# The first 512 columns of w_in in one pair of transfers, and the first chunk of batch 0's P in one run of 512 columns with both copies on ScalarE

## The chip, the cores and the metric

The kernel runs on one core of a Trainium2 chip. The metric is the device time of one execution in microseconds, as the median of several runs. Five engines work side by side: TensorE (PE in the profile, with its weight loads as PEld), VectorE (DVE), ScalarE (ACT), GpSimd (POOL) and SyncE (SP). Each takes its instructions in program order and waits at an instruction until the data and the buffers that it needs are there. Transfers are issued from the queues of POOL, SP and ACT, and run on 16 DMA engines.

## What is computed

Eight batches of attention between 512 tokens and 32 state vectors, in 8 heads of 64 columns, in both directions, and a dense block with an exact Gelu on the result:

```python
def _attn_ref(x, state):
    B, H, S, D = x.shape                    # 8, 8, 512, 64; state has 32 rows
    scale = 1.0 / np.sqrt(D)
    scores = scale * np.matmul(x, state.transpose(0, 1, 3, 2))
    ...
    a = np.exp(scores)
    a /= a.sum(-1, keepdims=True) + 1e-09
    xread = np.matmul(a, state)
    scores2 = scale * np.matmul(state, x.transpose(0, 1, 3, 2))
    ...
    sread = np.matmul(a2, x)
    return np.concatenate([xread, sread], axis=2)

def _moe_ref(x, w_in, w_out):               # x: 4352 x 512, w_in: 512 x 2048, w_out: 2048 x 512
    h = x @ w_in
    g = 0.5 * h * (1.0 + erf(h * inv_sqrt2))
    return g @ w_out
```

## The kernel before

**The product P.** For the token rows, `xread @ w_in` equals `a @ (state @ w_in)`, head by head. So the kernel first forms, for each batch, P = state @ w_in: a tile of 128 partitions by 2 halves t by 2048 columns, where half t holds four heads of 32 state rows each. It is made in chunks of 512 columns (`p_mm`, L435: for each of four head positions c and two halves t a matmul of 64 rows by 32 columns, so eight matmuls side by side) into two PSUM banks, and copied to SBUF as bf16. Then hp = P^T a^T gives 128 of the 2048 hidden columns for all 512 tokens at a time: two matmuls, t = 0 and t = 1, add into one bank (`mm1`, L501; for the first four of batch 0 `first`, L1112). ScalarE applies Gelu to hp and writes g, and TensorE multiplies g with w_out (`mm2_m`, L544, for batch 0).

**The start.** The order on every engine is written out by hand, from L1074 on. Batch 0 is loaded in four quarters q by SP and ScalarE queues as float32 and cast on chip; its scores, exponentials, sums and the normalized weights `a` follow quarter by quarter (`scores0`, `sums0`, `norm0`); `norm0(0)` gives the t = 0 half of `a`, `norm0(1)` the t = 1 half. `atr` (L363) transposes one half of `a` with four TensorE transposes into a PSUM bank; for batch 0 the t = 0 half is copied to SBUF (tile AT) by ScalarE and the t = 1 half by VectorE (L375, L376).

**The POOL queue.** All weights, the state of batches 1 to 7 and x of batches 1 to 7 are loaded through the POOL queue, with a cast from float32 to bf16 in the transfer. The order at the start is L126 to L131, then `load_x(1)` (L1096), then `load_rest` (L134). `load_w_in(f0, f1)` (L103) issues two transfers, one for each half t: 256 rows by f1 - f0 columns, which land on 64 partitions in four pieces each.

**The stretch around the change.** The first 512 columns of w_in come in two pairs of transfers of 256 columns. `pmat00(h)` (L480) makes half h of the first chunk of P of batch 0: eight matmuls of 256 columns into two PSUM tiles. On ScalarE it copies the t = 0 part, and for h = 0 the t = 1 part too. For h = 1 the t = 1 part stays in PSUM (`late`) until VectorE copies it at L1124, after the copy of AT's t = 1 half. Between these stand calls of `keep_warm(n)` (L146): matmuls on a tile of zeros, of n times 128 columns in all, that give TensorE work to do. After `first`, ScalarE runs the Gelu of four hp tiles (L1130), ahead of which the program loads ScalarE's table for that function.

**The PSUM banks.** Four banks, o0 to o3, are given out in turn by `otile` (L55) through a counter, `turn`; the next user of a bank waits until the one before has been read. Four more (`ftile`) hold hp and other products. Before `mm2_m(0, 0)` the counter is set to 3 (L1131).

**What follows.** From L1132 on: the products with w_out, a second burst of P chunks (`burst`, L1136, which needs w_in's columns 512 to 1024), then `xtr(1, ...)` (L1141), 32 TensorE transposes of x of batch 1, which need `load_x(1)` landed, and so on through the eight batches.

Of the kernel before, what the change touches and what calls it, by code (L numbers as in the profile page):

```python
# [10 lines left out]
BF16 = mybir.dt.bfloat16  # L11
# [6 lines left out]
def kernel(  # L18
# [8 lines left out]
    nc = tc.nc  # L27
# [3 lines left out]
    d_model, d_ff = moe_w_in.shape  # L31
    SB = S + NS
    scale = 1.0 / math.sqrt(D)
    HC = H // 2
# [6 lines left out]
    att = ctx.enter_context(tc.tile_pool(name="att", bufs=2))  # L41
# [11 lines left out]
    turn = [0]  # L53

    def otile(shape, name, at=None):  # L55
        if at is None:
            at = turn[0] % 4
            turn[0] += 1
        return ps_o.tile(shape, FP32, name=name, tag=f"o{at}")
# [6 lines left out]
    w_in_bf = persist.tile([128, HC, d_ff], BF16, name="w_in_bf")  # L66
    w_out_bf = persist.tile([128, MC, d_model], BF16, name="w_out_bf")
    ident = persist.tile([128, 128], BF16, name="ident")
    sbd = persist.tile([128, B, HC, 2 * NS], BF16, name="sbd")
# [33 lines left out]
    def load_w_in(f0, f1):  # L103
        for t in range(2):
            nc.gpsimd.dma_start(  # L105
                out=w_in_bf[64 * t:64 * t + 64, :, f0:f1],
                in_=moe_w_in[256 * t:256 * t + 256, f0:f1].rearrange("(c d) f -> d c f", c=HC),
            )
# [3 lines left out]
    def load_w_out(m0, m1):  # L112
        nc.gpsimd.dma_start(out=w_out_bf[:, m0:m1, :], in_=w_out_r[:, m0:m1, :])  # L113
# [9 lines left out]
            in_=st_rows[:, b0:b1, :, :].rearrange("q b t d -> q (b t) d"),  # L123
        )

    load_w_in(0, 256)  # L126
    load_w_in(256, 512)
    load_w_out(0, 2)
    load_st(1, 2)
    load_w_out(2, 4)  # L130
# [15 lines left out]
    def keep_warm(n):  # L146
        ps = otile([128, 512], "warm_ps")
        while n > 0:
            w = 128 * min(n, 4)
            nc.tensor.matmul(  # L150
                ps[:, 0:w], lhsT=warm[:, 0:128], rhs=warm[:, 0:w], start=True, stop=True
            )
            n -= 4
# [209 lines left out]
    def atr(b, ts=(0, 1)):  # L363
        A = atts[b]
        if 0 in ts:
            A.AT = att.tile([128, SJ, 2, 128], BF16, name="AT", tag="AT")
        for t in ts:
            if b == 0:
                ps = ps_o.tile([128, SJ, 128], BF16, name="aT_ps", tag=f"o{turn[0] % 4}")
                turn[0] += 1  # L370
            else:
                ps = ps_f.tile([128, SJ, 128], BF16, name="aT_ps", tag="f")
            for j in range(SJ):
                nc.tensor.transpose(ps[:, j, :], A.a[:, 2 * j + t, :], ident)
            copy = nc.scalar.copy if b == 0 and t == 0 else nc.vector.tensor_copy  # L375
            copy(out=A.AT[:, :, t, :], in_=ps)  # L376
# [56 lines left out]
    Ps = {}  # L433

    def p_mm(b, f, tiles):  # L435
        if b not in Ps:
            Ps[b] = att.tile([128, 2, d_ff], BF16, name="P", tag="P")
        ps = [tiles([128, 512], "p_ps") for t in range(2)]
        for c in range(HC):
            for t in range(2):  # L440
                nc.tensor.matmul(  # L441
                    ps[t][32 * c:32 * c + 32, :],
                    lhsT=sbd[64 * t:64 * t + 64, b, c, 32 * t:32 * t + 32],
                    rhs=w_in_bf[64 * t:64 * t + 64, c, f * 512:(f + 1) * 512],
                    start=True,
                    stop=True,
                )
        return ps
# [28 lines left out]
            p_copy(*x)  # L477


    def pmat00(h):  # L480
        if h == 0:
            Ps[0] = att.tile([128, 2, d_ff], BF16, name="P", tag="P")
        ps = [otile([128, 256], "p_ps") for t in range(2)]
        for c in range(HC):
            for t in range(2):
                nc.tensor.matmul(
                    ps[t][32 * c:32 * c + 32, :],
                    lhsT=sbd[64 * t:64 * t + 64, 0, c, 32 * t:32 * t + 32],
                    rhs=w_in_bf[64 * t:64 * t + 64, c, 256 * h:256 * h + 256],
                    start=True,  # L490
                    stop=True,
                )
        nc.scalar.copy(out=Ps[0][:, 0, 256 * h:256 * h + 256], in_=ps[0])
        if h == 0:
            nc.scalar.copy(out=Ps[0][:, 1, 0:256], in_=ps[1])
        return ps


    gs = {}
# [600 lines left out]
    norm0(1)  # L1100
    load_rest()
    keep_warm(2)
    pmat00(0)
    keep_warm(8)
    atr(0, (0,))
    keep_warm(4)
    late = pmat00(1)

    gs[0] = gpool.tile([128, MC, S], BF16, name="g", tag="g")
    hps = [ps_f.tile([128, S], FP32, name="hp", tag="f") for m in range(4)]  # L1110
# [10 lines left out]

    first(0, (0, 1))
    atr(0, (1,))
    nc.vector.tensor_copy(out=Ps[0][:, 1, 256:512], in_=late[1])  # L1124
    for q in range(4):
        ones0(q)
    first(0, (2, 3))
# [94 lines left out]
    for b in range(2, B):  # L1222
        nb = b + 1
        for p in range(8):
# [16 lines left out]
            late = p == 5 and b % 2 and nb < B  # L1241
# [115 lines left out]
```

## Time and profile before

| | us |
|---|---|
| median of 3 runs (lowest, highest) | 201.96 (201.9, 202.41) |
| the profiled execution | 202.25 |
| its span, from the first to the last instruction | 200.3 |
| TensorE busy | 193.9 (97%) |
| VectorE busy | 155.1 (77%) |
| ScalarE busy | 145.6 (73%) |
| GpSimd busy | 48.1 (24%) |
| granted TensorE clock | 1.00 in all of the span |

Each line of a timeline gives the start, the time taken, the engine, the line of the kernel, the operation, the tiles written and read, shapes and the number of instructions merged; in brackets the idle time before it and what ended it. Lines overlap, since matmuls are pipelined and an instruction can begin before the one ahead has been written back. "Us to landing" of a transfer runs from its issue to its arrival.

### The profile page before, as it was taken

The numbers are of one execution on the slowest core, as the hardware profiler recorded it, in microseconds if no ns is written. First come the engines' busy times: TensorE is split into PE (matmuls) and PEld (weight loads), VectorE is DVE, ScalarE is ACT, GpSimd is POOL, SyncE is SP. The second block draws the span as 40 slices with busy tenths as digits, with TensorE's granted clock in tenths as the row PEclk, the third lists the DMA queues.
The fourth block names the chain that finished last, engine by engine and source line by source line (L and its number), as shares of the span: only waits on it lengthen the run. The fifth ranks groups of instructions, "written<-read, shape, count | busy, mean of one in ns | idle before, by whom it ended". The sixth has DMA issues, their size and how long they took to land.

```text
span 200.3 us, 5055 instructions
## 1 busy us (share of the span) xinstructions
PE 193.9 (97%) x2102; PEld 134.3 (67%) x2107; DVE 155.1 (77%) x279; ACT 145.6 (73%) x264; POOL 48.1 (24%) x65
## 2 busy tenths in 40 slices
PE   7899999999999999999999999999999999999993
PEld 2533544465767777767777787677776888878893
DVE  2963796969989769975997798849966897984863
ACT  3785577699896799569966997599948778775120
POOL 8972504543403444040504300030000000000000
PEclk9999999999999999999999999999999999999999
DMA  5999999976494959680797025420024010030044
GB/s 192 197 174 202 206 199 201 183 136 142 84 149 77 241 65 164 141 214 0 77 188 209 5 67 95 138 75 27 28 107 106 0 55 0 7 153 0 18 146 157
DMA packets 40567, 23.16 MB, mean 116 GB/s; under 512 B 21856, under 2 KB 39136, under 8 KB 40544
## 3 DMA queue, kind: packets, MB, share of 16 engines
q0 software_dynamic: 13984, 8.10, 29.9%
q1 hardware_dynamic: 25728, 14.22, 27.5%
q10 hardware_dynamic: 832, 0.52, 0.8%
q8 instruction: 16, 0.26, 0.5%
q14 instruction: 7, 0.06, 0.1%
HBM read 17.30 MB, written 8.91 MB: 131 GB/s over the span
## 4 chain that ended last, share of the span: by engine, by line
PE 86%; DMA 5%; POOL 4%; ACT 2%; issue 0%; DVE 0%; POOLq 0%
PE xp L647 36%; PE hp L506 26%; DMA xb<-in_x_dram 5%; PE xp L727 5%; PE op L548 3%; PE sp L866 3%; PE rp L932 3%; POOL w_in_bf L105 2%; PE op L532 2%; PE xp L773 2%; PE pt L333 2%; ACT P L1002 1%; PE p_ps L441 1%; PE sr L962 1%; POOL sbd L95 1%; POOL w_out_bf L113 1%
## 5 line engine op out<-in xcount | busy, mean ns | idle before, releaser
L513 ACT ACTIVATE g<-hp 128x512 bf16<-128x512 f32 x124 | 67.1, 614 | 17.0 <-PE hp L506 16.8
L506 PE MATMUL hp<-AT,P 128*128 128x512 bf16 x248 | 62.2, 379 | 0.0
L647 PEld LDWEIGHTS <-gsum 128*128 128x128 bf16 x416 | 40.4, 98 | 8.9 <-issue 0.4
L647 PE MATMUL xp<-ws,gsum 128*128 128x256 bf16 x320 | 38.2, 273 | 0.0
L506 PEld LDWEIGHTS <-P 128*128 128x128 bf16 x248 | 23.0, 98 | 19.4 <-ACT P L452 0.7
L647 PEld LDWEIGHTS <-g 128*128 128x128 bf16 x240 | 23.3, 98 | 4.8
L637 DVE TENSOR_TENSOR gsum<-g 128x2048 bf16<-128x2048 bf16 x14 | 17.0, 1218 | 0.6 <-ACT g L513 0.6
L225 POOL COPY x<-xb 128x1024 bf16<-128x1024 bf16 x12 | 12.2, 1044 | 18.5 <-DMA xb<-in_x_dram 18.5
L235 POOL COPY xo<-xb 128x1024 bf16<-128x1024 bf16 x12 | 12.2, 1043 | 14.1 <-PE sr L962 13.9
L647 PE MATMUL xp<-w_out_bf,g 128*128 128x256 bf16 x128 | 15.3, 273 | 0.0
L647 PE MATMUL xp<-ws,g 128*128 128x256 bf16 x112 | 13.4, 273 | 0.0
L1016 POOL COPY hold<-g 128x1 bf16<-128x1 bf16 x7 | 2.3, 334 | 42.9 <-ACT g L513 42.9
L666 DVE TENSOR_TENSOR c<-qb 128x256 f32<-128x256 f32 x6 | 2.6, 425 | 12.7 <-ACT qb L749 12.7
L548 PE MATMUL op<-w_out_bf,g 128*128 128x512 bf16 x44 | 11.0, 380 | 0.5 <-issue 0.3
L647 PE MATMUL xp<-w_out_bf,gsum 128*128 128x256 bf16 x96 | 11.5, 273 | 0.0
L666 DVE TENSOR_TENSOR oh<-xp,c 128x512 f32<-128x512 f32 x14 | 9.6, 686 | 2.4 <-PE xp L647 2.0
L1002 DVE CAST P<-p_ps 128x512 bf16<-128x512 f32 x15 | 9.4, 683 | 2.4 <-PE p_ps L441 2.4
L356 DVE TENSOR_TENSOR a<-e,ics 128x512 bf16<-128x512 bf16 x14 | 10.5, 750 | 0.5
L353 DVE TENSOR_REDUCE cs<-e 128x16 f32<-128x512 bf16 x14 | 9.5, 678 | 0.9 <-ACT e L340 0.9
L513 ACT ACT_TABLE_LOAD x7 | 9.0, 1283 | 0.1
L441 PE MATMUL p_ps<-w_in_bf,sbd 64*32 64x512 bf16 x248 | 9.0, 380 | 0.0
L637 DVE TENSOR_TENSOR gsum<-gsum,g 128x2048 bf16<-128x2048 bf16 x7 | 8.6, 1225 | 0.2
(155 smaller groups left out, 308.9 us busy)
## 6 DMA issues: line engine op xcount, KB each, us to landing
out_dram<-oh SPq DMA_DIRECT2D x15, 256.0 KB, 3.3
xb<-in_x_dram POOLq DMA_DIRECT2D x7, 512.0 KB, 7.1
out_dram<-oh SPq DMA_DIRECT2D x6, 512.0 KB, 3.1
w_in_bf<-in_moe_w_in_dram POOLq DMA_DIRECT2D x6, 256.0 KB, 11.7
out_dram<-osb SPq DMA_DIRECT2D x5, 256.0 KB, 3.0
w_out_bf<-in_moe_w_out_dram POOLq DMA_DIRECT2D x4, 256.0 KB, 7.8
w_out_bf<-in_moe_w_out_dram POOLq DMA_DIRECT2D x2, 512.0 KB, 13.3
x0f<-in_x_dram SPq DMA_DIRECT2D x3, 256.0 KB, 3.8
```

The costliest lines, as they stand in the source:

```text
L225: nc.gpsimd.tensor_copy(out=A.x4[:, :, :, 64 * t:64 * t + 64].rearrange("p j c d -> p c j d"), in_=src[:, t],)
L235: eng.tensor_copy(out=A.xo[:, :, :, 2 + 64 * t:66 + 64 * t].rearrange("p j c d -> p c j d"), in_=src[:, t],)
L356: nc.vector.tensor_tensor(out=A.a[:, :, hs].rearrange("p g (c n) -> p g c n", n=NS), in0=e4, in1=ics[:, :, :].to_broadcast((128, G, 2, NS) ...
L441: nc.tensor.matmul(ps[t][32 * c:32 * c + 32, :], lhsT=sbd[64 * t:64 * t + 64, b, c, 32 * t:32 * t + 32], rhs=w_in_bf[64 * t:64 * t + 64, c ...
L506: nc.tensor.matmul(hp, lhsT=Ps[b][:, t, m * 128:(m + 1) * 128], rhs=atts[b].AT[:, :, t, :], start=(t == 0), stop=(t == 1),)
L513: nc.scalar.activation(out=gs[b][:, m, :], in_=hp, func=AF.Gelu)
L548: nc.tensor.matmul(ops[b, j], lhsT=gs[b][:, m, j * 128:(j + 1) * 128], rhs=w_out_bf[:, m, :], start=(m == 0), stop=(m == MC - 1),)
L637: nc.vector.tensor_tensor(out=got[name], in0=x, in1=y, op=op)
L647: nc.tensor.matmul(ps[:, j - js[0], :], lhsT=lhs[:, m, 128 * j:128 * j + 128], rhs=rhs[:, m, :], start=(first and j == js[0] and m == 0), ...
L666: nc.vector.tensor_tensor(out=out, in0=x, in1=y, op=ALU.add)
L727: nc.tensor.matmul(xs[b, 0][:, at, :], lhsT=lhs[:, m, :], rhs=rhs[:, m, :], start=(start and m == 0), stop=(m == MH // 2 - 1), skip_group_ ...
L1002: copy(out=Ps[b][:, t, f * 512:(f + 1) * 512], in_=ps[t])
```

## The change

`load_w_in(0, 512)` takes the place of `load_w_in(0, 256)` and `load_w_in(256, 512)`: two transfers on the POOL queue in place of four, each with twice as many columns. `pmat00` loses its argument: it calls `p_mm(0, 0, otile)`, so eight matmuls of 512 columns make the whole chunk, and ScalarE copies the t = 0 part at once. The t = 1 part stays in its bank until a second ScalarE copy, which now stands after the AT copy of the t = 0 half, so VectorE's copy at L1124 is gone. The counter `turn` is moved on by one, past the bank that holds this part. The warm-up matmuls, 12 times 128 columns in all, are four before and eight after `atr(0, (0,))`; before they were eight and four.

```diff
-    load_w_in(0, 256)
-    load_w_in(256, 512)
+    load_w_in(0, 512)
     load_w_out(0, 2)
     load_st(1, 2)
     load_w_out(2, 4)
@@
-    def pmat00(h):
-        if h == 0:
-            Ps[0] = att.tile([128, 2, d_ff], BF16, name="P", tag="P")
-        ps = [otile([128, 256], "p_ps") for t in range(2)]
-        for c in range(HC):
-            for t in range(2):
-                nc.tensor.matmul(
-                    ps[t][32 * c:32 * c + 32, :],
-                    lhsT=sbd[64 * t:64 * t + 64, 0, c, 32 * t:32 * t + 32],
-                    rhs=w_in_bf[64 * t:64 * t + 64, c, 256 * h:256 * h + 256],
-                    start=True,
-                    stop=True,
-                )
-        nc.scalar.copy(out=Ps[0][:, 0, 256 * h:256 * h + 256], in_=ps[0])
-        if h == 0:
-            nc.scalar.copy(out=Ps[0][:, 1, 0:256], in_=ps[1])
-        return ps
+    def pmat00():
+        ps = p_mm(0, 0, otile)
+        nc.scalar.copy(out=Ps[0][:, 0, 0:512], in_=ps[0])
+        return ps[1]
@@
     keep_warm(2)
-    pmat00(0)
+    late = pmat00()
+    keep_warm(4)
+    atr(0, (0,))
     keep_warm(8)
-    atr(0, (0,))
-    keep_warm(4)
-    late = pmat00(1)
+    nc.scalar.copy(out=Ps[0][:, 1, 0:512], in_=late)
+    turn[0] += 1
@@
     first(0, (0, 1))
     atr(0, (1,))
-    nc.vector.tensor_copy(out=Ps[0][:, 1, 256:512], in_=late[1])
     for q in range(4):
         ones0(q)
     first(0, (2, 3))
```

## The prediction

> **What bounds the kernel now.** I read the clock and span first (one core, span 200.3 us, granted clock 1.000), then the chain of work that ended last, the waits of TensorE, the timelines of the engines from 8 to 20 us, and the transfer rate by stretches. The profiled execution took 202.25 us, 1.95 us more than its span; the median of the runs is 201.96, so 0.29 us comes off any sum made in this profile.
>
> The chain, in order of time (start, us, what), where the change touches it:
>
> ```profile
> 3.05 2.65 POOL w_in_bf L105 x4
> 5.70 0.71 POOL w_out_bf L113
> ...
> 7.82 1.19 POOL w_in_bf L105 x2
> 9.01 10.36 DMA xb<-in_x_dram
> 19.36 0.04 issue
> 19.41 1.08 PE xT_ps L271 x32
> ```
>
> From 19.41 to the end the chain is TensorE almost throughout (86% of the span). Before that it runs through the POOL queue: four issues for w_in's first 512 columns, then five others, then the load of batch 1 of x, whose landing at 19.36 releases the transposes of batch 1. This looks as if 1.3 us less of POOL issue were worth 1.3 us. The waits of TensorE itself from 13 us to the end say otherwise (engine line, waited for, us in total, times, longest):
>
> ```profile
> PE op L548 <- issue: 0.3, 2, 0.2
> PE xT_ps L271 <- DMA xb<-in_x_dram: 0.2, 1, 0.2
> ```
>
> TensorE stood still for this landing for only 0.23 us (the timeline gives two digits: idle 19.18 to 19.41). However early the batch lands, no more than that 0.23 is won there. All else from 13.3 us on is work or waits for ScalarE and VectorE that move along with TensorE.
>
> What sets the time before 13.3 us: TensorE, ScalarE and VectorE in the stretch of the edit (start, us, what; in brackets the idle time before):
>
> ```profile
> 8.66 0.30 PE L486 MATMUL p_ps<-w_in_bf,sbd 64*32 64x256 bf16 x8
> ...
> 9.67 0.40 PE L374 MATMUL aT_ps<-ident,a 128*128 128x128 bf16 x4 [0.20 <-DVE a L315]
> ...
> 10.74 0.59 PE L1114 MATMUL hp<-AT,P 128*128 128x512 bf16 x2 [0.23 <-ACT AT L376]
> 11.34 0.40 PE L374 MATMUL aT_ps<-ident,a 128*128 128x128 bf16 x4
> 11.57 1.70 PE L1114 MATMUL hp<-AT,P 128*128 128x512 bf16 x6
> ```
>
> ```profile
> 10.11 0.58 ACT L376 COPY AT<-aT_ps 128x512 bf16<-128x512 bf16 x1 [0.43 <-PE aT_ps L374]
> 10.59 0.38 ACT L493 CAST P<-p_ps 128x256 bf16<-128x256 f32 x1
> 10.98 1.28 ACT L1130 ACT_TABLE_LOAD   x1
> 12.66 2.06 ACT L1130 ACTIVATE g<-hp 128x512 bf16<-128x512 f32 x4 [0.40 <-PE hp L1114]
> ```
>
> ```profile
> 10.59 0.69 DVE L315 TENSOR_TENSOR a<-e,ics 128x512 bf16<-128x512 bf16 x1
> 11.77 0.42 DVE L376 COPY AT<-aT_ps 128x512 bf16<-128x512 bf16 x1 [0.49 <-PE aT_ps L374]
> 12.12 0.41 DVE L1124 CAST P<-p_ps 128x256 bf16<-128x256 f32 x1
> ```
>
> The first Gelu starts at 12.66, and behind it stands a VectorE chain: the second normalization ends at 11.28, the four transposes start at 11.34, VectorE copies them by 12.19, the t = 1 matmuls of `first` close hp, Gelu starts. Neither P nor w_in is a link of it. P's copies have their own slack, which the sum below measures.
>
> **The change part by part.**
>
> *POOL.* Two of four w_in issues go: 4 took 2.70 us, so 0.68 each, and every later issue up to the load of batch 1 comes 1.35 us sooner (that one at 7.66, not 9.01). The issues that already wait for landings (at 14.44 and 15.69, each just after the landing of the transfer issued eight places before: 7.76 + 6.4 and 8.44 + 7.0) keep the same partners, since the whole row moves by two.
>
> *The transfers.* The same bytes go in pieces twice as long. Which is worth what depends on the rate (last column, GB/s; the stretch leads the line):
>
> ```profile
> 6.00:8.00 2.00, 1.62 (x26) 1.20 (x24) 1.83 (x6) 1.46 (x4) 2.00 (x4) 1.00 1.33 169
> 15.00:16.00 1.00, 1.00 (x7) 0.35 (x4) 0.44 (x2) 0.00 (x0) 0.36 (x2) 1.00 1.46 200
> 11.00:13.00 2.00, 1.91 (x12) 0.72 (x10) 1.51 (x6) 1.60 (x2) 1.88 (x4) 1.00 1.10 145
> ```
>
> While the four small w_in transfers run, the queues move 169 GB/s; later, with work piled up, 200; in one stretch 145 with work piled up too. The first w_in transfer (128 KB written) was issued at 3.00 and took 3.8 us to land: 6.8. The fourth was issued at 5.04 and took 4.1: 9.1. With two transfers of 256 KB the first needs 131 kB more behind 6.8, the second 262 kB behind that. At 200 GB/s that is 6.8 + 0.66 + 1.31 = 8.75; at 169, 9.1; at 145, 9.5. I take 8.75, because two issues of 0.68 us now bring 524 kB, 385 GB/s, so that issuing no longer holds the queues back; the bounds are 8.7 and 9.5. What stands behind the pair gains by the same reckoning: 524 kB take 3.1 us at 169 and 2.6 at 200, so everything later comes 0.5 us sooner (bounds: 0.5 later, at 145, and 1.35 sooner, the whole of the issue time). Batch 1 then lands at about 18.9 in place of 19.36, ahead of the 19.18 at which TensorE wants it: gain 0.23.
>
> [...]
>
> *TensorE.* Now the product needs both w_in transfers where it stands in the queue, at 8.66; before, it needed only the first half's pair, which had landed by 3.68 + 3.8 = 7.5. So a wait of about 0.1 us is added (8.75 against 8.66; bounds 0 and 0.85). Behind it on TensorE stand the warm-up, the transposes of a's t = 0 half and `first`; on ScalarE the copy of P's first half, the AT copy, the second P copy, the table load and Gelu. Eight matmuls of 512 columns take 0.41 us (the same eight at 24.94 in this trace) in place of 0.30 twice, so 0.19 less of TensorE work. With landing at L the run ends at L + 0.41, the warm-up of 4 at L + 0.63, and the transposes can start where they do now, 9.67, as long as L is under 9.04; they wait there for VectorE's `a` anyway (0.20 idle). Past that, the AT copy moves out, but the two matmuls at 10.74 are done 0.17 us before the transposes at 11.34 need the engine. So L up to about 9.2 costs nothing, and each us after it costs a us. At 8.75: nothing. At 9.5: 0.3.
>
> *ScalarE.* Three copies of 256 columns (0.37 to 0.38) become two of 512; the nearest, P L452, takes 0.585. P's first half: 9.2 + 0.6 = 9.8, before the AT copy is due at 10.11. The second: 10.59 to 11.18 instead of 10.97. The table load then ends at 12.46, not 12.26, and Gelu waits for hp until 12.66: the cover is the VectorE chain, 0.2 us of it left. If that chain were shorter, the full 0.2 would show. The t = 1 matmuls want this half of P only after 12.19.
>
> *VectorE.* The copy L1124 (0.41) goes; the four xo copies move up. They are used at 20.42, so nothing is won but a little ease for the last two t = 1 matmuls; Gelu works through hp at 0.52 each, so nothing follows.
>
> *PSUM.* The held bank is released at 11.2 and next written at 13.3; the second warm-up takes the bank that P's first copy frees at 9.8 and stands at 10.07. No wait.
>
> *Sum:* 0 before 13.3, -0.23 at 19.2, carried to the end. 200.3 - 0.23 + 1.95 = 202.02 in this profile, 201.73 against the median. I predict 201.7. A third of a per cent, 0.6 us, is what a measurement of this kernel can tell from no change; -0.23 is 0.1%.
>
> **The rivals.**
> *The pair lands late.* One transfer less in flight at the start, and the rate of the stretch 11 to 13 us (145) shows that longer pieces do not always go at 200. It decides from a landing of 9.2 on. At 145 GB/s: 0.3 us lost at the front; and batch 1 then lands 0.5 us later, at 19.9, where TensorE, itself 0.3 late, waits 0.4 rather than 0.23: together 0.5 us, 202.5. For it speaks that the time to spare is only 0.45 us; against, that even the old rate of 169 gives 9.1. With landing at 9.9 it would be 202.7 or more.
> *More than the visible wait is won.* If the weight loads of `first` that waited 0.24 us for the VectorE copy L1124 hold the Gelu chain, and the shorter TensorE work (0.19) shows, then -0.23 - 0.24 - 0.19 = -0.66: 201.3. Against it: Gelu starts before these matmuls are over, and TensorE idles for VectorE in this stretch.
> *The transfers gain nothing.* The queues are as full as before and batch 1 lands at 19.36 again: 201.96, no change. For it: the rate of 169 may come from the memory and not from the issuing.
>
> **How the numbers follow.** Forecast (-0.1 to -0.35 us): 0.42. Nothing gained (within 0.2 of before): 0.18. More than the visible wait: 0.21; late pair: 0.19. The first two lie within 0.3%; part of the third stays within too (0.03), and of the fourth (0.02), while 0.03 goes for faster and 0.03 for slower outcomes by delays of later transfers that I have not found. So faster 0.21, same 0.59, slower 0.20. The forecast's own range is 201.5 to 201.9. The whole: the low end reaches to the second rival, 201.3, less 0.1 for the spread of the runs; the high end to the late pair at 145 GB/s, 202.5, plus 0.1: 201.2 to 202.6.
>
> **What would show it.** Only two w_in issues ahead of the first w_out issue, which moves from 5.67 to about 4.3 us. The eight P matmuls start between 8.66 and 9.0, in one run of 0.4 us. AT's transposes still at 9.67 and the first Gelu at 12.66: a later Gelu means the late pair; an earlier one refutes the VectorE chain. Batch 1's transposes at 19.18 without a wait for the transfer. Two P copies on ScalarE of 0.59. I am wrong if TensorE's total idle time after 13 us was not what limited the gain, for instance if the span falls by more than 0.4 us with the first Gelu in place.

## The result, and the profile after

The changed kernel took 202.99 us (median of 20 runs, 202.12 to 205.07) against 202.12 us for the kernel before on the same chips (20 runs, 201.64 to 202.83). The ratio is 1.0056, with a 95% interval of 1.0032 to 1.0079: slower by about 0.6%, where 201.7 and a range of 201.2 to 202.6 had been forecast. The runs of the changed kernel fall into two groups. In 12 of the 20 TensorE's mean clock was 0.997 or more, and their median is 202.67 (one of them took 204.63, the others at most 203.06); in 8 it was 0.989 to 0.992, and they took 203.39 to 205.07. The profiled execution, 204.12 us with a span of 202.0, is of the second group. Ratios leave out executions over 1.5% above the fastest of the same kernel; medians and counts take them all.

The changed kernel's timelines from 6 to 22 us (start, us, engine, line and operation, in brackets the idle time before): TensorE first.

```profile
6.83 0.29 PE L291 MATMUL pc<-sb,xT 128*128 128x64 bf16 x4
9.02 0.61 PE L256 MATMUL xT_ps<-ident,x0b 128*128 128x128 bf16 x4 [1.90 <-DVE x0b L242]
...
10.84 0.63 PE L440 MATMUL p_ps<-w_in_bf,sbd 64*32 64x512 bf16 x8
...
21.28 1.08 PE L270 MATMUL xT_ps<-ident,xb 128*64 128x128 bf16 x32
```

VectorE, ScalarE and POOL:

```profile
6.35 0.42 DVE L260 COPY xT<-xT_ps 128x512 bf16<-128x512 bf16 x1
8.40 0.56 DVE L242 CAST x0b<-x0f 128x512 bf16<-128x512 f32 x1 [1.62 <-DMA x0f<-in_x_dram]
```

```profile
11.53 0.59 ACT L481 CAST P<-p_ps 128x512 bf16<-128x512 f32 x1 [0.41 <-PE p_ps L440]
12.46 0.59 ACT L375 COPY AT<-aT_ps 128x512 bf16<-128x512 bf16 x1 [0.34 <-PE aT_ps L373]
12.94 0.59 ACT L1093 CAST P<-p_ps 128x512 bf16<-128x512 f32 x1
13.55 1.28 ACT L1116 ACT_TABLE_LOAD   x1
14.84 2.06 ACT L1116 ACTIVATE g<-hp 128x512 bf16<-128x512 f32 x4
```

```profile
3.00 1.43 POOL L105 DMA_DIRECT2D w_in_bf<-in_moe_w_in_dram  x2
4.42 0.72 POOL L113 DMA_DIRECT2D w_out_bf<-in_moe_w_out_dram  x1
...
7.76 0.95 POOL L117 DMA_DIRECT2D xb<-in_x_dram  x1
```

And its rate and clock by stretches (third value from the end: the granted clock; last: GB/s):

```profile
6.00:7.00 1.00, 1.00 (x17) 0.76 (x17) 0.74 (x2) 0.82 (x4) 1.00 (x2) 1.00 0.76 86
...
9.00:10.00 1.00, 0.98 (x9) 0.77 (x10) 0.62 (x2) 0.12 (x1) 0.65 (x1) 0.50 1.34 196
10.00:11.00 1.00, 1.00 (x15) 0.53 (x13) 0.93 (x4) 0.53 (x2) 0.40 (x2) 0.50 1.35 202
```

The reader is to see four things. POOL does what the change says: the first w_out issue is at 4.42 and the load of batch 1 at 7.76. Between 6 and 7 us the transfers move only 86 GB/s, where the kernel before had 168. In this execution the last quarter of batch 0's own x, which SP's queue loads, then took 6.6 us to land and not the 4.6 that was the longest in the profile before; VectorE waits 1.62 us for it, TensorE 1.90, and after that gap TensorE's clock is granted by half for 3.4 us (worked out from the rows of 8 to 13 us: 0.93, 0.50 three times, 0.86). And batch 1's transposes no longer wait for their load. The second w_in transfer landed at 10.3 (issued at 3.7, 6.6 us), but that cost nothing in this execution, since TensorE came to P's matmuls only at 10.84.

All the loss lies ahead of the first Gelu. From it to batch 1's transposes the changed kernel takes 21.28 - 14.84 = 6.44 us; before it was 19.41 - 12.66 = 6.75. So a small gain like the one that was forecast there is seen, 0.31 us; and from those transposes to the end both take the same within 0.2 (202.0 - 21.28 = 180.7; before 180.9).

### The profile page after: what moved, and what is told of

The parts are those of the page before. It is cut to its first block, busy times and chain, and to the rows that moved or that the text cites. A ratio compares the mean times of both kernels' runs of the same rounds, so it can differ in the third digit from the quotient of the medians.

```text
span 202.0 us, 5035 instructions
## 1 busy us (share of the span) xinstructions
PE 194.5 (96%) x2095; PEld 134.8 (67%) x2099; DVE 155.2 (77%) x278; ACT 145.7 (72%) x263; POOL 49.9 (25%) x63
## 3 DMA queue, kind: packets, MB, share of 16 engines
q0 software_dynamic: 13440, 8.10, 29.7%
## 4 chain that ended last, share of the span: by engine, by line
PE 91%; DMA 3%; ACT 3%; DVE 1%; issue 1%; SPq 0%
PE xp L633 36%; PE hp L492 27%; PE op L534 5%; PE xp L713 5%; DMA x0f<-in_x_dram 3%; PE sp L852 3%; PE rp L918 3%; PE p_ps L440 2%; PE op L518 2%; PE xp L759 2%; PE pt L332 2%; ACT P L988 1%; PE sr L948 1%; PE hp L1101 1%; PE warm_ps L149 1%; ACT g L499 1%
## 5 line engine op out<-in xcount | busy, mean ns | idle before, releaser
L224 POOL COPY x<-xb 128x1024 bf16<-128x1024 bf16 x12 | 15.3, 1303 | 17.1 <-DMA xb<-in_x_dram 17.1
L534 PE MATMUL op<-w_out_bf,g 128*128 128x512 bf16 x45 | 11.3, 380 | 0.3 <-issue 0.2
L355 DVE TENSOR_TENSOR a<-e,ics 128x512 bf16<-128x512 bf16 x14 | 9.9, 708 | 0.5
L440 PE MATMUL p_ps<-w_in_bf,sbd 64*32 64x512 bf16 x256 | 9.7, 387 | 0.0
```

The costliest lines, as they stand in the source:

```text
L224: nc.gpsimd.tensor_copy(out=A.x4[:, :, :, 64 * t:64 * t + 64].rearrange("p j c d -> p c j d"), in_=src[:, t],)
L355: nc.vector.tensor_tensor(out=A.a[:, :, hs].rearrange("p g (c n) -> p g c n", n=NS), in0=e4, in1=ics[:, :, :].to_broadcast((128, G, 2, NS) ...
L440: nc.tensor.matmul(ps[t][32 * c:32 * c + 32, :], lhsT=sbd[64 * t:64 * t + 64, b, c, 32 * t:32 * t + 32], rhs=w_in_bf[64 * t:64 * t + 64, c ...
L534: nc.tensor.matmul(ops[b, j], lhsT=gs[b][:, m, j * 128:(j + 1) * 128], rhs=w_out_bf[:, m, :], start=(m == 0), stop=(m == MC - 1),)
```

## The experiments

Eleven kernels, and the changed kernel once more (e4); each ratio is against runs of the kernel before on the same chip. "Halved" counts the executions with a mean clock of 0.992 or less. In e6 to e8, e10 and e11 the first chunk of P gets other values, so these kernels serve only to time the waits and the transfers.

**The two parts alone, and the changed kernel again.**

```diff
 e1: the kernel before, with
-    load_w_in(0, 256)
-    load_w_in(256, 512)
+    load_w_in(0, 512)
 e2: the changed kernel, with
-    load_w_in(0, 512)
+    load_w_in(0, 256)
+    load_w_in(256, 512)
 e3: the changed kernel, with load_w_in(0, 512) as two calls of
+    in_=moe_w_in[256 * t + 64 * c0:256 * t + 64 * c1, 0:512]   # c0:c1 = 0:2, 2:4
```

> The kernel before with only the transfers changed: one pair of 512 columns of w_in, P still in two halves with the copies as before. In the profile of the changed kernel the last quarter of batch 0's x reached VectorE at 8.40 us instead of 6.90, TensorE stood still for 1.90 us and its clock was halved for 3.4 us after it. Theory A (the long w_in transfers hold up the last pieces of x0f): as slow as the changed kernel, 202.7 to 203.2, with some executions at a mean clock of about 0.992. Theory B (the new order of P's matmuls and ScalarE copies costs the time): as before, 202.1, all executions at 1.00.

> The changed kernel with its four w_in transfers of 256 columns given back; P in one run of 512 columns, both copies on ScalarE. Theory A: as before, 202.1 (or 0.2 less, since 0.19 us of TensorE work is gone), clock 1.00. Theory B: 202.7 to 203.2.

> The changed kernel with the same 512 columns in four transfers, each with all 512 columns of half the rows (pieces of 512 columns, 128 KB written for each issue). If it is the long pieces that hold up x0f: as slow as the changed kernel, 202.9. If it is the amount that one issue puts in the queues: as before, 202.1. Theory B: 202.9 as well, but then the compute alone is slow too.

> The changed kernel once more, on the same chip as the three others, for its spread and for a second profile. Theory A: two kinds of executions, those at clock 1.00 with a span near 200.4 and those near 0.992 with a span of 201.3 or more; a profile of the first kind shows the last quarter of x0f in time.

| kernel | median us | ratio, 95% interval | halved |
|---|---|---|---|
| e1 transfers alone | 202.56 | 1.0033 (1.0008 to 1.0058) | 3 of 12 |
| e2 compute alone | 202.71 | 1.0037 (1.0016 to 1.0057) | 2 of 12 |
| e3 rows in halves | 202.96 | 1.0041 (1.0020 to 1.0061) | 3 of 12 |
| e4 changed again | 202.97 | 1.0052 (1.0024 to 1.0081) | 5 of 12 |
| before (with these) | 202.06 | | 0 of 35 |

Neither theory A (a late x0f) nor theory B (the order of the copies) fits: each part alone is slow. At full clock the medians lie 0.44 (e1), 0.62 (e2) and 0.57 us (e4) above the kernel before, so the two together cost no more than the dearer of them. The second profile of the changed kernel, e4, shows a third thing, because its x0f came in time. Its TensorE, and its rate from 6 to 7 us:

```profile
8.46 0.37 PE L440 MATMUL p_ps<-w_in_bf,sbd 64*32 64x512 bf16 x1
9.89 0.41 PE L440 MATMUL p_ps<-w_in_bf,sbd 64*32 64x512 bf16 x7 [1.06 <-DMA w_in_bf<-in_moe_w_in_dram]
```

```profile
6.00:7.00 1.00, 1.00 (x17) 0.65 (x14) 0.92 (x4) 0.82 (x3) 1.00 (x2) 1.00 0.77 79
```

The first of P's eight matmuls reads the first transfer's half and starts; the second needs the other transfer and waits 1.06 us. Issued at 3.7, that transfer took 6.1 us, so it landed at 9.8. The same wait is there in the other two parts, e1 (idle 0.49 and 0.94) and e2:

```profile
10.09 0.30 PE L485 MATMUL p_ps<-w_in_bf,sbd 64*32 64x256 bf16 x7 [0.94 <-DMA w_in_bf<-in_moe_w_in_dram]
```

```profile
9.98 0.41 PE L441 MATMUL p_ps<-w_in_bf,sbd 64*32 64x512 bf16 x7 [0.30 <-DMA w_in_bf<-in_moe_w_in_dram]
```

This is theory C: before, P's first half needed only the first two of four small transfers. With either part of the change, P's first matmuls need all 512 columns, and these are not there before 9 us, with two transfers or with four. This fits that the parts don't add. Four issues are late in another way than two: in e2 and e3 the fourth is issued at 5.0 and takes 4.9 and 4.8 us, with 147 and 154 GB/s from 6 to 7 us. e3's row:

```profile
6.00:7.00 1.00, 0.97 (x16) 0.61 (x13) 0.99 (x4) 0.83 (x3) 1.00 (x2) 1.00 1.10 154
```

So e3, which reads the changed kernel's pieces by half the rows, is as slow in time (202.96), but not in its rate.

**A filler in the wait, and the wait taken away.**

```diff
 e5: the changed kernel, with
-    keep_warm(2)
+    keep_warm(14)
     late = pmat00()
 e6: the changed kernel, and e8: the kernel before, in P's matmuls for the first chunk of batch 0
-    rhs=w_in_bf[64 * t:64 * t + 64, c, ...],
+    rhs=warm[64 * t:64 * t + 64, ...],
 e7: the changed kernel, in the first pair of transfers
-    in_=moe_w_in[256 * t:256 * t + 256, 0:512].rearrange("(c d) f -> d c f", c=HC)
+    in_=moe_w_out[256 * t:256 * t + 256, 0:512].rearrange("(c d) f -> d c f", c=HC)
```

> The changed kernel with 12 times 128 columns more of warm-up right before P's matmuls (0.64 us of TensorE work laid into the wait for w_in, which was 1.06 us in the last profile of the changed kernel). Two parts are to be told apart: the wait itself, and the halved clock that follows it in some executions. If the halved clock comes from TensorE standing idle in that wait: no or nearly no executions at 0.992 or below any more, the median falls to about 202.5, the fastest executions stay at 202.1 to 202.4. If the halved clock comes from something else (the late x0f, say): the same spread as before, 202.9.

> The changed kernel, with the first chunk of batch 0's P multiplied from a tile of zeros in place of w_in's first 512 columns: all transfers and all instructions stay, only the wait of P's matmuls for the landing of w_in is gone. Theory C (the product now waits for all 512 columns, which land after 9 us): the first Gelu is back near 12.3 to 12.7, batch 1's transposes start near 19.2 without a wait, no halved clock, 201.7 to 201.9, a little under the kernel before. Theory A (the long transfers hold up x0f): still 202.7 to 203.0 with executions at 0.992.

> The changed kernel with the first pair of transfers reading the first 512 rows of w_out (whole rows of 512 columns, one right behind the other in memory) in place of w_in's first 512 columns (pieces of 512 columns, one row of 2048 apart): the same pieces, bytes and places on the chip, another pattern in memory; the values of the first chunk of P are others. In the profiles of the changed kernel the rate fell to 79 to 110 GB/s between 6 and 7 us, and the pair landed at 9.8 to 10.0. If the pattern of w_in makes the slump: 190 GB/s or more from 6 to 7 us, the pair lands at about 8.8, the wait is gone, 201.8 to 202.0. If the slump comes from the start of the queue or from the end of x0f: as the changed kernel, 202.9.

> The kernel before, with both halves of batch 0's first chunk of P multiplied from a tile of zeros: the control for the same edit of the changed kernel. P's first half doesn't wait in the profile of before, so 202.0, as before, under either theory; if it is well under that, the kernel before waits for w_in as well in a part of its executions.

| kernel | median us | ratio, 95% interval | halved |
|---|---|---|---|
| e5 filler | 203.34 | 1.0052 (1.0022 to 1.0083) | 3 of 12 |
| e6 P of zeros | 201.68 | 1.0000 (0.9968 to 1.0032) | 3 of 12 |
| e7 w_out's rows | 201.92 | 0.9986 (0.9970 to 1.0002) | 0 of 12 |
| e8 before, P of zeros | 202.39 | 1.0017 (0.9991 to 1.0042) | 1 of 10 |
| before (with these) | 202.28 | | 2 of 35 |

e6 bears theory C out. With all transfers in place and only the wait gone, the other 9 executions have a median of 201.66, 8 of them between 201.55 and 201.74, and the profile looks as the forecast had it (P's matmuls; batch 1's transposes):

```profile
8.42 0.41 PE L484 MATMUL p_ps<-warm,sbd 64*32 64x512 bf16 x8
...
18.87 1.08 PE L270 MATMUL xT_ps<-ident,xb 128*64 128x128 bf16 x32
```

Those 201.66 lie about 1.0 us under the 202.67 (202.63 in e4) of the changed kernel's executions at full clock, and 1.2 us when each is taken against the kernel before on its own chip (0.62 under it, 0.57 above it): that is the price of the wait. The ratio over e6 is no better than before because three executions with a halved clock remain (204.22 to 205.28), so not all of these come from the wait. The control e8 shows no gain: the kernel before does not wait for w_in.

e7 changes nothing but where the pair reads, and shows why it is late. The rate, and P's matmuls:

```profile
6.00:7.00 1.00, 0.68 (x12) 0.47 (x11) 1.00 (x3) 0.71 (x3) 1.00 (x2) 1.00 1.24 205
```

```profile
8.72 0.42 PE L444 MATMUL p_ps<-w_in_bf,sbd 64*32 64x512 bf16 x8
```

205 GB/s, the second transfer 4.9 us after its issue at 3.8, so at 8.7, and no wait. The prediction's sum for a rate of 200 was 8.75.

e5 did not do what was expected: the gap shrank (0.27 us left in its profile), but 3 of 12 executions still had a halved clock and the median did not fall. So it is not shown that the idle time in P's wait is what halves the clock.

**Which pattern in memory is slow.**

```diff
 e9: the changed kernel, four transfers in place of the pair
+    w_in_r = moe_w_in.rearrange("(t c d) f -> t c d f", t=2, c=HC)
+    for c in range(HC):
+        nc.gpsimd.dma_start(out=w_in_bf[:, c, 0:512], in_=w_in_r[:, c, :, 0:512])
 e10: the changed kernel, in the first pair
-    .rearrange("(c d) f -> d c f", c=HC)
+    .rearrange("(d c) f -> d c f", c=HC)
 e11: the changed kernel, in the first pair
-    in_=moe_w_in[256 * t:256 * t + 256, 0:512]
+    in_=moe_w_in.rearrange("d (g f) -> (d g) f", f=512)[256 * t:256 * t + 256, :]
```

> The changed kernel with w_in's first 512 columns in four transfers, one for each head position c: 128 rows of 512 columns (pieces one row of 8 KB apart, no jump of 64 rows from piece to piece), landing in the order in which P's matmuls take them. If the jumps of 512 KB from piece to piece make the slump of 6 to 7 us: the rate there is 190 GB/s or more, the last of the four lands near 9.0, TensorE waits for at most 0.3 us, 201.7 to 202.1, no halved clock. If rows 8 KB apart are enough to make it: 80 to 155 GB/s, 202.7 to 203.0.

> The changed kernel with the pair of transfers reading the same 512 rows and 512 columns of w_in in another order: head position c of partition d takes row 4d + c of its half, not row 64c + d (the values of the first chunk of P are others). Pieces read one after another are 8 KB apart in place of 512 KB; two issues, bytes and places on the chip as in the changed kernel. If the jumps of 512 KB make the slump: as with w_out's rows, 205 GB/s, the pair lands at 8.6, 201.8 to 202.1, no halved clock. If it is that w_in's pieces are not contiguous: as the changed kernel, 202.9, with halved clocks.

> The changed kernel with the first pair of transfers reading w_in's memory as one contiguous megabyte (pieces of 512 columns one right behind the other: the first 128 rows whole, in place of 512 columns of 512 rows; the values of the first chunk of P are others). It parts the pattern from the place: if pieces 8 KB apart make the slump, 190 GB/s or more from 6 to 7 us, the pair at 8.6, no wait of TensorE for it, 201.7 to 202.1, no halved clock, as with w_out's rows. If it is w_in's place in memory: 79 to 110 GB/s, 202.9, with halved clocks.

| kernel | median us | ratio, 95% interval | halved |
|---|---|---|---|
| e9 four by c | 210.00 | 1.0383 (1.0344 to 1.0422) | 6 of 6 |
| e10 row order | 203.38 | 1.0059 (1.0031 to 1.0086) | 4 of 9 |
| e11 w_in contiguous | 201.93 | 1.0014 (0.9984 to 1.0043) | 3 of 12 |

The rate from 6 to 7 us, of e10 and of e11:

```profile
6.00:7.00 1.00, 0.96 (x17) 0.71 (x16) 0.87 (x3) 0.82 (x3) 1.00 (x2) 1.00 0.80 83
```

```profile
6.00:7.00 1.00, 1.00 (x17) 0.64 (x14) 1.00 (x4) 0.83 (x3) 1.00 (x2) 1.00 1.22 201
```

e11 parts the pattern from the place: the same tensor read as one contiguous piece of memory goes at 201 GB/s, the pair is there at 8.9, TensorE waits 0.29 us, and the executions at full clock have a median of 201.8. e10 shows that it is not the jumps of 512 KB: pieces 8 KB apart, in order, go at 83 GB/s. So pieces of 2 KB that stand one row of 8 KB apart are read slowly here when two issues bring them; the four issues of e3, with the same pieces, had 154. What the number of issues does to the rate is not shown. e9 says nothing on the pattern and met neither forecast. Its rate was 27 GB/s from 6 to 7 us and its POOL queue moved 17056 packets in place of 13440, so the four transfers were of another make. What made them so is not shown.

**A version that hides the wait.** P's matmuls stand behind the transposes of the t = 0 half of `a`, and the table for Gelu is loaded early:

```diff
-    keep_warm(2)
+    nc.scalar.activation(out=spare, in_=spare, func=AF.Gelu)
+    keep_warm(14)
+    atr(0, (0,))
     late = pmat00()
     keep_warm(4)
-    atr(0, (0,))
-    keep_warm(8)
     nc.scalar.copy(out=Ps[0][:, 1, 0:512], in_=late)
-    turn[0] += 1
```

> The changed kernel with the wait moved to where it is covered: P's matmuls stand behind the transposes of a's t = 0 half (the warm-up ahead of them), the AT copy comes before both P copies on ScalarE, and ScalarE's table for Gelu is loaded early by one Gelu of a single column, behind the last exponential. By theory C a landing of w_in up to about 10.1 then costs little: first Gelu at 12.7 to 13.0, batch 1's transposes without a wait, median 201.8 to 202.1, that is level with the kernel before or 0.2 under it; executions with a late x0f and a halved clock stay (a third of them), since the slump stays. If theory C is wrong: 202.9.

Measured 202.53 (ratio 1.0039, 1.0006 to 1.0072; halved 3 of 12) against 202.01 for the kernel before on this chip, so slower, and a miss. ScalarE and TensorE in its profile:

```profile
9.19 1.28 ACT L1088 ACT_TABLE_LOAD   x1
10.49 0.20 ACT L1088 ACTIVATE spare<-spare 128x1 f32<-128x1 f32 x1
10.60 0.57 ACT L375 COPY AT<-aT_ps 128x512 bf16<-128x512 bf16 x1
11.06 0.59 ACT L481 CAST P<-p_ps 128x512 bf16<-128x512 f32 x1
```

```profile
10.13 0.41 PE L440 MATMUL p_ps<-w_in_bf,sbd 64*32 64x512 bf16 x8
...
11.71 0.61 PE L1100 MATMUL hp<-AT,P 128*128 128x512 bf16 x2 [0.85 <-ACT P L481]
```

The wait for w_in is gone, but P's copy now stands behind the table load and the AT copy, and `first` waits 0.85 us for it. The wait only changed its name. No other version was tried, and none that beats the kernel before is shown.

## Why the prediction was wrong, step by step

**The step that failed** is the landing of the pair: "At 200 GB/s that is 6.8 + 0.66 + 1.31 = 8.75 ... I take 8.75, because ... issuing no longer holds the queues back; the bounds are 8.7 and 9.5." It landed at 9.8 in e4 and 10.3 in the profile of the result, and TensorE resumed at 10.09 in e1, beyond even the upper bound. The rate of 200 was taken from a stretch where other data was under way; at the start, with w_in's pieces, it was 79 (e4), 86 and 110 GB/s (e1) from 6 to 7 us. With contiguous pieces the same sum held (8.7 in e7, 8.9 in e11). The row that had warned of it, 145 GB/s, was in the prediction, and was used as a bound and not as a likely value.

**What followed had the right mechanism.** The late pair was the first rival, with a landing of 9.2 from which each us costs a us. The time at which the last of P's waiting matmuls start against the first Gelu bears that out, in the profiles where the clock stayed whole:

| | P's last matmuls | first Gelu | 12.66 + (start - 9.2) | batch 1's transposes | span |
|---|---|---|---|---|---|
| before | 8.66 (first half) | 12.66 | | 19.41 | 200.3 |
| e3 | 9.87 | 13.23 | 13.33 | 19.67 | 200.4 |
| e2 | 9.98 | 13.36 | 13.44 | 19.80 | 200.6 |
| e1 | 10.09 | 13.57 | 13.55 | 20.01 | 200.7 |
| e5 | 9.84 | 13.21 | 13.30 | 19.65 | 200.4 |
| e6 | 8.42 | 12.43 | | 18.87 | 199.6 |
| e7 | 8.72 | 12.72 | | 19.16 | 199.9 |
| e11 | 8.97 | 12.35 | | 18.79 | 199.6 |

The first Gelu of e6 and e11 is earlier than 12.66 because VectorE's second normalization ended at 11.05 and 10.92 there, and not at 11.28. The prediction had taken the 9.2 from TensorE's line alone. In e2 and e3 ScalarE's line is just as long: P's copy, the AT copy, the second P copy, the table load and Gelu follow one another without a gap, and Gelu comes 3.38 us after P's last matmuls (e2), so by that line 9.28 is the last start without a cost (12.66 - 3.38). That this lies so near 9.2 was luck.

**What was not priced** is the clock. The prediction gave the wait a us for a us. In e4 the clock was halved from 11.3 us on (0.63 in the row of 11 to 12 us, 0.50 in the next; its mean of 0.992 over 201.5 us comes to 3.0 to 3.4 us at half), and the first Gelu came at 14.38, 1.0 us after the 13.35 that the wait alone gives (12.66 + 9.89 - 9.2):

```profile
12.00:13.00 1.00, 1.00 (x7) 0.72 (x6) 0.00 (x0) 1.00 (x1) 0.41 (x1) 0.50 1.23 203
```

```profile
14.38 1.57 ACT L1116 ACTIVATE g<-hp 128x512 bf16<-128x512 f32 x3 [1.13 <-PE hp L1101]
```

With 8 of 20 executions so, the median is 202.99 and not 202.67. What brings such a stretch on is not shown. In the 3.4 us ahead of the drop TensorE worked for 1.4 us in the profile of the result, 1.6 us in e10 and 2.0 us in e4. But e1 has 3.4 us that are as empty (1.7 us of work from 8.4 to 11.8) and keeps its clock (1.00 in every row from 2 to 13 us). e5 and e6 speak against the wait alone: with a gap of 0.27 us in the one profile and none in the other, 3 of 12 executions were halved in each.

**What was not foreseen at all** is that SP's load of x0f can suffer: in the profile of the changed kernel its last quarter landed 2 us late. In e2 (5.5 us; TensorE idle for 1.12 us) and e8 (5.4 us), which both have the four transfers, it is late too, so this is not tied to the pair. How many of the halved executions a late x0f makes is open, and e7, 0 of 12, and e11, 3 of 12, both without the slump, do not agree on it.

**Right were** the POOL times (4.3 and 7.66 forecast, 4.42 and 7.76 seen) and the cover of the second P copy by the VectorE chain (0.2 forecast; in e6 Gelu still waits 0.18 us for hp behind the table load). That VectorE's dropped copy would win nothing holds as well: in e6, as before, Gelu starts 0.47 us after VectorE has copied AT.

**Right in size, but not shown in its cause,** is the gain at batch 1's load (0.23 forecast; from 6.75 to 6.44 us between Gelu and the transposes in e1, e2, e3, e6 and the changed kernel alike, so 0.31). e2 and e8, with the old four transfers, show 6.44 and 6.43 too, without a wait for that load. e2 issues it at 8.90, close to the 9.01 of the kernel before; POOL, which waits for it later, got on at 18.43 there and at 19.65 before. So the wait that the change was to save is not in every execution of the old transfers.

**The whole sum with the pair in time.** e7 lies 0.28 us under the kernel before by its ratio (0.9986, 0.9970 to 1.0002), e11 0.23 us by its executions at full clock (201.78 against 202.01), where 0.23 had been forecast; neither is clear of noise. e6 lies 0.62 us under the kernel before on its chip (201.66 against 202.28), more than the sum gives, and why is open. That its 201.66 is close to the 201.7 of the forecast is luck of the chip.

## What to carry to other kernels

Merging two runs of a matrix product also merges what they wait for: the first half inherits the landing of the second (here 9.8 us in e4, where the first pair of before was there by 7.5), so look at the landing before looking at the instructions saved. Here the rate of a transfer went with the pattern that it reads (from 6 to 7 us 83 GB/s in e10, 201 in e11) and with when it runs (e1: 110 from 6 to 7 us, 203 from 11 to 13), so take it from a row with the same pattern at a like point in time, or let the slow row be the likely case. And where TensorE's wait falls into the start-up, count a possible stretch at half the clock beside it: here 8 of 20 executions were halved, for 3.4 us in the profile of the result, though what brings that on is not shown.

## What the runs showed of the hardware that was not expected

- Pieces of 2 KB read at a pitch of 8 KB, as the first work of the POOL queue: from 6 to 7 us 83 GB/s (e10) and 72 to 128 in the changed pair (72 in e12, 128 in e5), 154 when four issues bring them (e3), against 201 to 205 for contiguous pieces of the same size (e11, e7). With the next pair of the same shape under way, all transfers together moved 198 to 205 GB/s from 11 to 16 us in the profile of the result, where it was issued at 6.5 and 7.2 and landed at 14.4 and 15.8 (e1: 202 to 204 from 11 to 13 us). In the kernel before, where this pair is the first with such pieces (issued at 7.8 and 8.4, landed at 14.2 and 15.4), they moved 145 from 11 to 13 us and 191 to 200 from 13 to 16. In e7 and e11, whose first pair is contiguous, the rate from 11 to 13 us is 163 and 171, against 203 in e1. So the slump seems to go with the first such pair; why is open.
- A mean clock of 0.992 or less, in the profile of the result 3.4 us at half the clock, in 8 of 20 executions of the changed kernel (5 of 12 in e4) and in 3 of 107 of the kernel before (0 of 35, 2 of 35, 1 of 14 and 0 of 23 beside the experiments). The eight took 0.7 to 2.4 us more than the median of the other twelve.
- Beside the slump, a transfer of another queue came late: x0f's last quarter, 6.6 us from issue to landing in place of 4.6 in the profile of the result. Without the pair the longest x0f transfer took 5.5 (e2) and 5.4 us (e8). That the slump makes it late is not shown.
